# A retention and ELU kernel: a gate before the first weight load, PSUM tiles of the turn split by copying engine, and a redrawn order around the value scaling

## The chip, the cores and the metric

The kernel runs on one core of a Trainium2 chip. The metric is the device time of one execution in microseconds (us). TensorE (PE in the profile) multiplies matrices, VectorE (DVE), ScalarE (ACT) and GpSimd (POOL) do elementwise work, and SyncE (SP) issues DMAs. DMAs are issued from SyncE, GpSimd and, for some outputs, ScalarE; they share the core's 16 DMA engines. Those that convert float32 to bfloat16 on the way are issued from GpSimd. PE writes its results to PSUM, from which VectorE and ScalarE read.

## The reference

Retention over 8 batches of 8 heads, 576 positions and a head size of 64, followed by a two-layer network with an ELU between the layers, on 4608 tokens of 512 features (hidden size 2048):

```python
scores = scale * np.matmul(q, k.transpose(0, 1, 3, 2))
gamma = 1.0 - 2.0 ** (-5.0 - np.arange(H, dtype=np.float32))
rel = pos[:, None] - pos[None, :]
Dmat = np.where(rel >= 0, gamma[:, None, None] ** rel[None, :, :], 0.0)
attn = np.matmul(scores * Dmat[None], v)               # B, H, S, D
x = attn.transpose(0, 2, 1, 3).reshape(B * S, H * D)
h = x @ w_in
g = np.where(h > 0.0, h, np.exp(np.minimum(h, 0.0)) - 1.0)
out = g @ w_out
```

## The kernel before, in words

The 4608 tokens are 36 units of 128. The decay factors into a part for the keys, which is multiplied into the values (`gk`, `gkp`), and a part for the queries, which is multiplied into the attention output (`gx`); within a unit a 0/1 mask is applied to the scores, and across units a running state of 64 by 64 per head is carried. The attention output `xt` is already turned, so that it feeds the first layer as it is. Units form groups of at most four. `f1(g, n)` is a tile of the first layer for group g: matmuls with `w_in_sb` into a PSUM bank `ph` (L544), then on ScalarE `e = exp(ph)` (L549), on GpSimd `m = e - 1` (L551) and on VectorE `g = min(max(ph, 0), m)` (L524). The second layer multiplies `g` by `w_out_sb` (L569, L600), copies, and stores. A bank of `ph` is free again once its `g` is made.

The order of instructions on every engine is the order in which the program writes them. Each engine works through its own queue strictly in that order, so an instruction that waits holds up what stands behind it on its engine; the tile layer puts the waits in. VectorE's `g` is written three tiles after its matmuls (`finish(3)` in `tick`), so that its place among VectorE's other work follows from the order of the `f1` calls.

The change concerns the first four units. They are handled as two pairs: pair 0 is units 0 and 1, pair 1 is units 2 and 3, each with 256 positions of the first sequence in all 8 heads. What happens to a pair s:

- its keys and queries are loaded. For pair 0 in float32 on SyncE, two halves of four heads each (`rawk`, `rawq`, L130), and cast to bfloat16 by VectorE (first half) and ScalarE (second half), L625 to L630. For pair 1 directly as bfloat16 on GpSimd (`pair_qk`, L119);
- its values are loaded in float32 (`pair_v`, L124): on SyncE for pair 0, on GpSimd for pair 1, each in two halves;
- `pair_scale` (L358, GpSimd) multiplies the values by the keys' decay, two instructions;
- `pair_turn_in(s, c)` (L375) turns the keys (c = 1) or queries (c = 0) on PE in two parts a = 0, 1 of eight transposes each, and `pair_turn_out` (L383, L385) copies a part to SBUF, with `V` (VectorE) or `A` (ScalarE). Before the change all four parts of a pair stand in one PSUM tile `tr`, and the tile layer orders the engines that touch it;
- `pair_scores(s, a)` (L397) multiplies queries by keys into `psc`, and VectorE masks the result (L403) to `ppt`; a = 0 uses the PSUM tag "o", a = 1 the tag "sc";
- `pair_states` (L415) and `pair_state_out` (L444, L440 on ScalarE) make the states, `pair_intra` (L468) and `pair_inter` (L457) the outputs, and `pair_x` (L479, VectorE) the x of the pair, on which group s of the first layer starts.

Between them PE runs dummy matmuls (`dummy`, L218) on a tile of zeros. The weights are loaded on GpSimd: `load_w_in(n)` (L105) brings a quarter of w_in, enough for four 128-wide hidden tiles, in two DMAs; `load_w_out` (L108) half of w_out in one. `f1(0, 0)` and `f1(0, 1)` use quarter 0, `f1(0, 2)` and `f1(0, 3)` quarter 1, `f1(0, 4)` and `f1(0, 5)` quarter 2; quarter 3 and w_out are used after the first eight tiles of groups 0 and 1. There are three `ph` banks; a tile that names `m` uses the bank "pm" in place of one.

The PSUM pools: "ph" of three banks, "pm" of one, "sc" and "o" of two banks each, all handed out in turn, with a wait until the last reader of the previous user is done.

Of the kernel before, what the change touches and what calls it, by code (L numbers as in the profile page):

```python
# [9 lines left out]
FP32 = mybir.dt.float32  # L10
BF16 = mybir.dt.bfloat16
# [6 lines left out]
def kernel(  # L18
# [9 lines left out]
    nc = tc.nc  # L28
    PSUM = bass.MemoryType.PSUM

    B, H, S, D = q.shape
    DM, DF = moe_w_in.shape
    P = 128
    HP = H // 2
# [24 lines left out]
    const = ctx.enter_context(tc.tile_pool(name="const", bufs=1))  # L59
# [10 lines left out]
    ps_h = ctx.enter_context(tc.tile_pool(name="ps_h", bufs=3, space=PSUM))  # L70
    ps_m = ctx.enter_context(tc.tile_pool(name="ps_m", bufs=1, space=PSUM))
    ps_s = ctx.enter_context(tc.tile_pool(name="ps_s", bufs=1, space=PSUM))
    ps_o = ctx.enter_context(tc.tile_pool(name="ps_o", bufs=1, space=PSUM))
# [28 lines left out]
    def load_w_in(n):  # L102
        s = slice(n * 512, (n + 1) * 512)
        for b in range(2):
            nc.gpsimd.dma_start(w_in_sb[b * 64 : b * 64 + 64, :, s], w_in_v[b, :, :, s])  # L105

    def load_w_out(f0, f1):
        nc.gpsimd.dma_start(w_out_sb[:, f0:f1], w_out_v[:, f0:f1])  # L108
# [3 lines left out]
    def pair_runs(x, s, h0, h1):  # L112
        return x[0, h0:h1, 2 * P * s : 2 * P * (s + 1), :].rearrange("h (p e) d -> p h (e d)", e=2)

    pq, pk_, pv, pvn, pT, ppt, pst = {}, {}, {}, {}, {}, {}, {}

    def pair_qk(s, x, kept):
        kept[s] = qkpool.tile([P, H, 2 * D], BF16, name="pqk", tag="qkn")
        nc.gpsimd.dma_start(kept[s], pair_runs(x, s, 0, H))  # L119

    def pair_v(s, queue):
        pv[s] = [raw.tile([P, HP, 2 * D], FP32, name="pv", tag="rv") for b in range(2)]
        for b in range(2):
            queue.dma_start(pv[s][b], pair_runs(v, s, b * HP, (b + 1) * HP))  # L124


    rawk, rawq = ([opool.tile([P, HP, 2 * D], FP32, name="rqk", tag="ot") for b in range(2)] for c in range(2))
# [15 lines left out]
    for h in range(H):  # L143
        b, j = divmod(h, KJ)
# [25 lines left out]
    for c in range(2):  # L170
        nc.gpsimd.iota(
            pk_i[c * 64 : (c + 1) * 64, R + 4 : R + 6], pattern=[[1, 2]], base=-MID, channel_multiplier=2
        )
    load_w_in(0)
    pair_qk(1, q, pq)
    pair_qk(1, k, pk_)
    pair_v(1, nc.gpsimd)

    pk = const.tile([P, R + 6], FP32, name="pk")
    nc.vector.tensor_copy(pk, pk_i)  # L180
    ident = const.tile([P, P], BF16, name="ident")
# [30 lines left out]
    def dummy(n, bank=None):  # L212

        if n:
            pool, tag = bank or (ps_m, "pm")
            dum = pool.tile([P, 512], FP32, name="dum", tag=tag)
        for _ in range(n):
            nc.tensor.matmul(dum, warm[:, :P], warm, start=True, stop=True)  # L218
# [136 lines left out]
    def pair_scale(s):  # L355
        pvn[s] = [nat.tile([P, HP, 2, D], BF16, name="pvn", tag="vn") for b in range(2)]
        for b in range(2):
            nc.gpsimd.tensor_tensor(  # L358
                pvn[s][b], pv[s][b].rearrange("p h (e d) -> p h e d", e=2),
                gkp[:, s, b * HP : (b + 1) * HP].unsqueeze(3).to_broadcast([P, HP, 2, D]), ALU.mult,  # L360
            )

    def pair_turn_in(s, c):


        if (s, "tr") not in pT:
            pT[s, "tr"] = ps_s.tile([P, 2, 2, 2, 2, P], BF16, name="tr", tag="sc")
            pT[s] = [tpool.tile([P, 2, 2, 2 * P], BF16, name="pT", tag="qkT") for a in range(2)]
        n = (pq, pk_)[c][s]
        for a in range(2):  # L370
            part = pT[s, "tr"][:, a, c] if s == 0 else pT[s, "tr"][:, c, a]
            for j in range(2):
                for e in range(2):
                    for b in range(2):
                        nc.tensor.transpose(  # L375
                            part[b * D : (b + 1) * D, j, e], n[:, b * HP + 2 * a + j, e * D : (e + 1) * D], ident
                        )

    def pair_turn_out(s, c, a, copy):

        part = pT[s, "tr"][:, a, c] if s == 0 else pT[s, "tr"][:, c, a]
        if c:
            copy(pT[s][a][:, 1], part.rearrange("p j e t -> p j (e t)"))  # L383
        else:
            copy(pT[s][a][:, 0].rearrange("p j (t e) -> p j e t", e=2), part)  # L385

    def pair_scores(s, a):

        pool, tag = ((ps_o, "o"), (ps_s, "sc"))[a]
        sc = pool.tile([P, 2, 2, 2, P], FP32, name="psc", tag=tag)  # L390
        t = pT[s][a]
        for j in range(2):
            for e in range(2):
                for c in range(2):
                    for b in range(2):
                        r = slice(b * D, (b + 1) * D)
                        nc.tensor.matmul(  # L397
                            sc[c * 64 : (c + 1) * 64, b, j, e],
                            t[r, 1, j, e * P + c * 64 : e * P + (c + 1) * 64], t[r, 0, j, c * P : (c + 1) * P],
                            start=(j == 0 and e == 0), stop=(j == 1 and e == 1), skip_group_check=True,  # L400
                        )
        pt = ppool.tile([P, 2, 2, 2, P], BF16, name="ppt", tag="pt")
        nc.vector.tensor_tensor(  # L403
            pt.rearrange("p b j e t -> p (b j) e t"), sc.rearrange("p b j e t -> p (b j) e t"),
            maskp.unsqueeze(1).to_broadcast([P, 4, 2, P]), ALU.mult,
        )
        ppt[s, a] = pt

    def pair_state(out, s, rows, layout, first):

        for j in range(HP):
            for e in range(2):
                for b in range(2):
                    h = 4 * b + j if layout == "b" else 2 * j + b
                    nc.tensor.matmul(  # L415
                        out[b * D : (b + 1) * D, j], pk_[s][rows, h, e * D : (e + 1) * D],
                        pvn[s][h // HP][rows, h % HP, e],
                        start=(first and j == 0 and e == 0), stop=(j == HP - 1 and e == 1), skip_group_check=True,
                    )

    def pair_states(s):

        unit = slice(0, 64)
        if s == 0:
            pst[1] = ps_h.tile([P, HP, D], FP32, name="pst", tag="ph")
            both = ps_m.tile([P, 2, HP, D], FP32, name="pst2", tag="pm")
            pst[2], pst[4] = both[:, 0], both[:, 1]
            pst[3] = pst[2]
            pair_state(pst[1], 0, unit, "b", True)
            pair_state(pst[2], 0, slice(0, P), "b", True)  # L430
            pair_state(pst[4], 0, slice(0, P), "", False)
        else:
            pair_state(pst[3], 1, unit, "b", False)
            pair_state(pst[4], 1, slice(0, P), "", False)

    def pair_state_out(u):

        if u == 4:
            sbs[u] = ppool.tile([P, HP, D], BF16, name="sb", tag="sb")
            nc.scalar.copy(sbs[u], pst[u])  # L440
            return
        for b in range(2):
            r = slice(b * D, (b + 1) * D)
            nc.scalar.copy(sbd[u - 1][r, :, r], pst[u][r])  # L444

    def pair_outputs(s):
        if s == 0:
            for u in range(2):
                os_[u] = ps_h.tile([P, HP, P], FP32, name="po", tag="ph")
        else:  # L450
            o = ps_o.tile([P, 2, HP, P], FP32, name="po", tag="o")
            os_[2], os_[3] = o[:, 0], o[:, 1]
# [22 lines left out]
    def pair_x(s):  # L475
        xts[s] = xpool.tile([P, KJ, 512], BF16, name="xt", tag="xt")
        for c in range(2):
            s0 = (2 * s + c) * P
            nc.vector.tensor_tensor(  # L479
                xts[s][:, :, c * P : (c + 1) * P], os_[2 * s + c], gx[:, :, s0 : s0 + P], ALU.mult  # L480
            )
# [135 lines left out]
    h, m = (ps_h, "ph"), (ps_m, "pm")  # L617
# [5 lines left out]
    spare = (ps_o, "o")  # L623
# [11 lines left out]
    pair_turn_out(0, 0, 0, V)  # L635
    pair_turn_out(0, 0, 1, A)
    pair_scale(0)
    for n in range(1, 4):
        load_w_in(n)
    pair_scale(1)  # L640
    dummy(3, spare)
    pair_scores(0, 0)
    pair_scores(0, 1)
    make_gx(2, 3)
# [13 lines left out]
    def f1(g, n, bank=None):  # L658
        k = 512 // (P * len(GROUPS[g]))
        ffn1(g, k * n, bank, (g, n) == (0, 0))  # L660
# [4 lines left out]
    for c, copy in ((1, V), (0, A)):  # L665
        for a in range(2):
            pair_turn_out(1, c, a, copy)
    f1(0, 1)
    load_w_out(0, 8)
    load_w_out(8, 16)  # L670
    pair_scores(1, 0)
    pair_states(1)
    pair_state_out(3)
    pair_scores(1, 1)
    f1(0, 2)
    pair_outputs(1)
    pair_intra(1, 0)
    pair_inter(2)
# [1 line left out]
    pair_inter(3)  # L680
    pair_x(1)
    pair_state_out(4)
    f1(0, 3)
    f1(0, 4, m)
    f1(0, 5)
    make_mask()
# [51 lines left out]
    for g in range(3, NG + 1):  # L738
# [6 lines left out]
        a, b = 0, 1 if g == 4 else 0  # L745
# [80 lines left out]
```

## Time and profile before

| what | value |
|---|---|
| median of 4 runs | 317.09 us |
| lowest and highest run | 316.65 and 318.78 us |
| the profiled execution: time and span | 316.79 us and 315.0 us |
| PE, PE weight loads | 304.2 us (97%), 167.8 us (53%) |
| VectorE, ScalarE, GpSimd | 179.8 (57%), 126.2 (40%), 198.5 us (63%) |
| DMA moved | 41.12 MB, mean 131 GB/s |
| gaps of PE over 0.6 us after its first instruction | 2.71 us ahead of 10.12, 0.69 ahead of 22.82, 1.23 ahead of 76.37 |

The span is from the first to the last instruction; the time of a run has what lies around it too. Lines such as L375 are lines of the kernel before; in the changed kernel they stand a few lines lower. In the timeline and in the chain of waits the first number is the start in us, the second the duration; in brackets stands how long the engine was idle ahead of the instruction and what ended that. In the windows each row is a stretch of time with each engine's busy time and number of instructions, then the granted PE clock as a share of full speed, the DMA share and GB/s.

### The profile page before, as it was taken

How to read it: one execution, taken by the hardware profiler on the slowest of the kernel's cores; microseconds unless marked ns; L12 is line 12 of the kernel's file. 1: busy time of each engine (PE TensorE's matmuls, PEld its weight loads, DVE VectorE, ACT ScalarE, POOL GpSimd, SP SyncE). 2: the span in 40 equal slices, each digit the busy share in tenths (PEclk: the TensorE clock that was granted, in tenths of full speed). 3: DMA queues.
4: the chain of work that ended last, by engine and by line, in shares of the span. 5: the costliest groups of instructions: out<-in, count | busy, mean ns of one | idle time of the engine just before them, and what ended most of it. 6: DMA issues, size and time to landing. Idle time of an engine off the chain costs nothing.

```text
span 315.0 us, 7512 instructions
## 1 busy us (share of the span) xinstructions
PE 304.2 (97%) x3006; PEld 167.8 (53%) x3006; DVE 179.8 (57%) x303; ACT 126.2 (40%) x229; POOL 198.5 (63%) x287
## 2 busy tenths in 40 slices
PE   7799999998999999999999999999999999999995
PEld 2377745876766555555444444444444444444444
DVE  5339625686766777577666555565556555434300
ACT  4445602442443444344434433444344433444411
POOL 8276887697977878877777666776664433333300
PEclk9599999999999999999999999999999999999999
DMA  7999999999999999999999999999996200000111
GB/s 160 218 168 164 200 127 186 191 137 184 213 154 172 153 165 154 160 126 159 143 144 133 144 134 135 133 135 134 115 154 85 67 35 35 35 33 33 69 67 68
DMA packets 145827, 41.12 MB, mean 131 GB/s; under 512 B 133632, under 2 KB 141184, under 8 KB 145792
## 3 DMA queue, kind: packets, MB, share of 16 engines
q0 software_dynamic: 73184, 13.64, 53.8%
q1 hardware_dynamic: 71168, 24.72, 42.2%
q10 hardware_dynamic: 1440, 2.29, 2.3%
q8 instruction: 23, 0.38, 0.5%
q14 instruction: 12, 0.10, 0.1%
HBM read 36.70 MB, written 9.44 MB: 146 GB/s over the span
## 4 chain that ended last, share of the span: by engine, by line
PE 87%; DMA 4%; DVE 4%; ACT 1%; POOL 1%; issue 1%; SPq 0%; ACTq 0%; POOLq 0%; DVEq 0%
PE ph L544 35%; PE pm L569 33%; PE pm L600 4%; PE o L349 3%; PE sc L261 3%; DMA rqk<-in_q_dram 2%; DMA qkT<-qkn 2%; PE dum L218 1%; POOL m L551 1%; DVE g L524 1%; PE o L300 1%; PE o L316 1%; PE pmh L585 1%; DVE pt L278 1%; PE tr L375 1%
## 5 line engine op out<-in xcount | busy, mean ns | idle before, releaser
L551 POOL TENSOR_SCALAR m<-e 128x512 bf16<-128x512 f32 (+1 forms) x152 | 90.3, 596 | 89.9 <-ACT e L549 81.5
L544 PE MATMUL ph<-xt,w_in_sb 128*128 128x512 bf16 (+3 forms) x840 | 145.8, 312 | 0.8 <-DVE rv L82 0.4
L549 ACT ACTIVATE e<-ph 128x512 f32<-128x512 f32 (+1 forms) x152 | 87.3, 575 | 142.0 <-PE ph L544 134.3
L524 DVE SCALAR_TENSOR_TENSOR g<-ph,m 128x512 bf16<-128x512 f32 (+1 forms) x152 | 99.5, 659 | 60.9 <-POOL m L551 60.8
L569 PE MATMUL pm<-w_out_sb,g 128*128 128x512 bf16 x496 | 125.6, 379 | 0.2 <-ACT ot L576 0.2
L544 PEld LDWEIGHTS <-w_in_sb 128*128 128x128 bf16 x840 | 74.3, 98 | 52.3 <-issue 1.7
L569 PEld LDWEIGHTS <-g 128*128 128x128 bf16 x496 | 48.0, 98 | 53.1 <-issue 0.4
L491 DVE TENSOR_TENSOR xt<-o,gx 128x512 bf16<-128x512 f32 x32 | 22.1, 690 | 35.9 <-PE o L316 30.6
L278 DVE TENSOR_TENSOR pt<-sc,mask 128x1024 bf16<-128x1024 f32 x32 | 38.9, 1214 | 3.1 <-PE sc L261 3.1
L226 POOL TENSOR_TENSOR vn<-rv,gk 128x512 bf16<-128x512 f32 x32 | 33.3, 1041 | 3.0 <-PE ph L544 1.9
L93 POOL DMA_DIRECT2D qkn<-in_q_dram x36 | 32.1, 893 | 0.7 <-DVE pt L278 0.4
L93 POOL DMA_DIRECT2D qkn<-in_k_dram x36 | 30.7, 853 | 0.0
L576 ACT COPY ot<-pm 128x512 f32<-128x512 f32 x31 | 18.1, 585 | 14.1 <-PE pm L569 14.1
L261 PEld LDWEIGHTS <-qkT 64*64 64x64 bf16 x512 | 8.0, 106 | 13.1 <-issue 10.5
L261 PE MATMUL sc<-qkT 64*64 64x128 bf16 (+1 forms) x512 | 13.2, 211 | 1.4 <-DMA qkT<-qkn 1.2
L600 PE MATMUL pm<-w_out_sb,g 128*128 128x512 bf16 x64 | 14.5, 379 | 0.0
L349 PE MATMUL o<-pt,vn 128*64 128x128 bf16 x256 | 13.2, 225 | 0.0
L218 PE MATMUL dum<-warm 128*128 128x512 bf16 x26 | 10.5, 556 | 1.2 <-DVE warm L136 1.2
L300 PE MATMUL o<-qkT,sb 64*64 64x128 bf16 (+1 forms) x232 | 10.2, 215 | 0.4 <-DVE rv L82 0.4
L600 PEld LDWEIGHTS <-g 128*128 128x128 bf16 x64 | 6.1, 98 | 6.8 <-issue 0.2
L349 PEld LDWEIGHTS <-vn 128*64 128x64 bf16 x256 | 8.1, 109 | 2.7
L316 PE MATMUL o<-vn,qkn 128*64 128x64 bf16 (+1 forms) x224 | 8.2, 196 | 0.0
(76 smaller groups left out, 113.9 us busy)
## 6 DMA issues: line engine op xcount, KB each, us to landing
rv<-in_v_dram SPq DMA_DIRECT2D x28, 256.0 KB, 5.0
out_dram<-ot SPq DMA_DIRECT2D x27, 256.0 KB, 2.4
qkn<-in_q_dram POOLq DMA_DIRECT2D x28, 128.0 KB, 5.3
qkn<-in_k_dram POOLq DMA_DIRECT2D x28, 128.0 KB, 5.2
w_in_sb<-in_moe_w_in_dram POOLq DMA_DIRECT2D x8, 256.0 KB, 7.3
w_out_sb<-in_moe_w_out_dram POOLq DMA_DIRECT2D x2, 1024.0 KB, 12.2
out_dram<-ot ACTq DMA_DIRECT2D x8, 256.0 KB, 4.9
rv<-in_v_dram SPq DMA_DIRECT2D x8, 128.0 KB, 4.1
```

Of the source, the lines that this page charges most:

```text
L93: nc.gpsimd.dma_start(kns[u][p0 : p0 + n, c], (q, k)[c][b, :, s0 : s0 + n, :].rearrange("h p d -> p h d"))
L226: nc.gpsimd.tensor_tensor(vns[u], raws[u], gk[:, u % R].unsqueeze(2).to_broadcast([P, H, D]), ALU.mult)
L261: nc.tensor.matmul(sc[j * 64 : (j + 1) * 64, i, hp, c], t[r, 1, hp, j * 64 : (j + 1) * 64], t[r, 0, hp, c], start=(hp == 0), stop=(hp == H ...
L278: nc.vector.tensor_tensor(pts[u][:, s].rearrange("p i h t -> p (i h) t"), scs[u][:, s].rearrange("p i h t -> p (i h) t"), m.unsqueeze(1).t ...
L349: nc.tensor.matmul(o[b * D : (b + 1) * D, i, a * P : (a + 1) * P], vns[u][:, h], pts[u][:, i, 2 * b + a], start=(u % R == 0 and a == 0), s ...
L491: nc.vector.tensor_tensor(xts[g][:, :, i * P : (i + 1) * P].rearrange("p (a i) t -> p a i t", a=2), outputs(os_[u]), gx[:, :, s0 : s0 + P] ...
L524: nc.vector.scalar_tensor_tensor(gt_, ph, 0.0, m, ALU.max, ALU.min)
L544: nc.tensor.matmul(ph[:, i * n + c : i * n + c + step], w_in_sb[:, j, f : f + P], xts[g][:, j, c : c + step], start=(j == 0), stop=(j == K ...
L549: nc.scalar.activation(e[:, w], ph[:, w], AF.Exp)
L551: nc.gpsimd.tensor_scalar(m[:, w], e[:, w], -1.0, 1.0, ALU.add, ALU.mult)
L569: nc.tensor.matmul(pm, gts[g, ft][:, it * P : (it + 1) * P], w_out_sb[:, ft], start=(ft == 0), stop=(ft == NFT - 1))
L600: nc.tensor.matmul(acc[u], gts[g, ft][:, it * P : (it + 1) * P], w_out_sb[:, ft], start=(ft == 0), stop=(ft == NFT - 1))
```

## The change

- A one-element copy on GpSimd, `gate`, reads the second half of pair 0's keys, ahead of the first `load_w_in`. GpSimd's following instructions stand behind it.
- `pair_v(1)` on GpSimd moves from behind the `pair_qk` loads to behind `pair_scale(0)`.
- Of the three `load_w_in` behind it, quarters 1 and 2 stay ahead of `pair_scale(1)`; quarter 3 moves ahead of `f1(0, 1)`. The halves of w_out move from behind `f1(0, 1)` to behind `f1(0, 2)` and behind `f1(0, 3)`.
- The turned parts of a pair no longer share one PSUM tile. Pair 0: the two parts of the keys are tiles of "ph", those of the queries are tiles of "sc" (copied by VectorE) and "o" (copied by ScalarE). Pair 1: the keys stand in "sc" (both copied by VectorE), the queries in "o" (both copied by ScalarE).
- `dummy(3, spare)` ahead of the first scores moves to the bank "pm".
- For pair 1 the second scores follow the first directly, ahead of the states; `f1(0, 2)` moves from behind them to behind `pair_x(1)`. With that the first `g` on VectorE stands behind `pair_x(1)`, not ahead of it.

```diff
@@
+    gate = const.tile([1, 1], FP32, name="gate")
+    nc.gpsimd.tensor_copy(gate, rawk[1][0:1, 0, 0:1])
     load_w_in(0)
     pair_qk(1, q, pq)
     pair_qk(1, k, pk_)
-    pair_v(1, nc.gpsimd)
@@ def pair_turn_in(s, c):
         if (s, "tr") not in pT:
-            pT[s, "tr"] = ps_s.tile([P, 2, 2, 2, 2, P], BF16, name="tr", tag="sc")
+            pT[s, "tr"] = {}
             pT[s] = [tpool.tile([P, 2, 2, 2 * P], BF16, name="pT", tag="qkT") for a in range(2)]
         n = (pq, pk_)[c][s]
+        sc, o, h = (ps_s, "sc"), (ps_o, "o"), (ps_h, "ph")
         for a in range(2):
-            part = pT[s, "tr"][:, a, c] if s == 0 else pT[s, "tr"][:, c, a]
+            pool, tag = (h if c else (sc, o)[a]) if s == 0 else (sc if c else o)
+            if s == 0 or a == 0:
+                part = pool.tile([P, 2, 2, 2, P], BF16, name="tr", tag=tag)
+            pT[s, "tr"][c, a] = part[:, a if s else 0]
...
 def pair_turn_out(s, c, a, copy):
-        part = pT[s, "tr"][:, a, c] if s == 0 else pT[s, "tr"][:, c, a]
+        part = pT[s, "tr"][c, a]
@@
     pair_scale(0)
-    for n in range(1, 4):
-        load_w_in(n)
+    pair_v(1, nc.gpsimd)
+    load_w_in(1)
+    load_w_in(2)
     pair_scale(1)
-    dummy(3, spare)
+    dummy(3, m)
     pair_scores(0, 0)
@@
             pair_turn_out(1, c, a, copy)
+    load_w_in(3)
     f1(0, 1)
-    load_w_out(0, 8)
-    load_w_out(8, 16)
     pair_scores(1, 0)
+    pair_scores(1, 1)
     pair_states(1)
     pair_state_out(3)
-    pair_scores(1, 1)
-    f1(0, 2)
     pair_outputs(1)
     pair_intra(1, 0)
     pair_inter(2)
@@
     pair_x(1)
     pair_state_out(4)
+    f1(0, 2)
+    load_w_out(0, 8)
     f1(0, 3)
+    load_w_out(8, 16)
     f1(0, 4, m)
```

More of the change, by code (lines that the diff above doesn't have):

```diff
@@ L375, in pair_turn_in @@
                         nc.tensor.transpose(
-                            part[b * D : (b + 1) * D, j, e], n[:, b * HP + 2 * a + j, e * D : (e + 1) * D], ident
+                            pT[s, "tr"][c, a][b * D : (b + 1) * D, j, e],
+                            n[:, b * HP + 2 * a + j, e * D : (e + 1) * D], ident,
                         )
     def pair_turn_out(s, c, a, copy):
-        part = pT[s, "tr"][:, a, c] if s == 0 else pT[s, "tr"][:, c, a]
+        part = pT[s, "tr"][c, a]
         if c:
```

## The prediction

> All times are microseconds from the start of the profiled span of the kernel before. "Front" is everything up to the turn of the second pair (the first 32 transposes of L375 that start at 20.07), "back" is from there to the fourth tile of the first layer, f1(0,3).
>
> **What bounds the kernel now.** I read the page's slices first: TensorE is at 97%, nearly full from the fourth slice to the last, so a change can pay only where TensorE has gaps or runs slowly, and the slices put both into the first 30 us. Then the chain of waits, in order of time:
>
> ```profile
> 2.33 6.62 DMA rqk<-in_q_dram
> ...
> 8.97 0.62 ACT pqk L630
> 9.59 0.49 ACT pT L383
> ...
> 10.12 1.07 PE tr L375 x16
> ...
> 12.64 1.07 PE psc L397 x28
> 13.71 1.82 PE dum L218 x4
> 15.53 0.73 PE po L468 x14
> ```
>
> The start hangs on the second half of the first pair's q, which is 6.62 us under way. The dummies before 15.53 hide another wait, shown by the timeline of GpSimd: the second value tile is only scaled at 14.57, after its DMA.
>
> ```profile
> 14.57 1.04 POOL L358 TENSOR_TENSOR pvn<-pv,gk 128x512 bf16<-128x512 f32 x1 [0.60 <-DMA pv<-in_v_dram]
> ```
>
> Next the view of DMA issues, one issue at a time (last column: issue to landing), and the windows of 1 us (last columns: granted clock, DMA share, GB/s):
>
> ```profile
> rqk<-in_k_dram SPq DMA_DIRECT2D x1, 256.0 KB, 2.9
> rqk<-in_q_dram SPq DMA_DIRECT2D x1, 256.0 KB, 6.6
> pv<-in_v_dram SPq DMA_DIRECT2D x1, 256.0 KB, 11.1
> pqk<-in_k_dram POOLq DMA_DIRECT2D x1, 256.0 KB, 11.8
> ```
>
> ```profile
> 3.00:4.00 1.00, 1.00 (x4) 0.34 (x3) 0.74 (x4) 0.84 (x2) 0.99 (x3) 1.00 1.08 313
> 4.00:5.00 1.00, 1.00 (x3) 0.30 (x2) 0.92 (x3) 0.49 (x1) 1.00 (x2) 1.00 0.94 266
> 6.00:7.00 1.00, 1.00 (x19) 0.59 (x18) 0.20 (x2) 0.00 (x0) 1.00 (x2) 1.00 0.79 126
> 10.00:11.00 1.00, 0.88 (x16) 0.82 (x15) 0.00 (x0) 0.07 (x1) 0.00 (x0) 0.50 1.24 212
> ```
>
> SyncE's queue alone moves some 276 GB/s (249, 313 and 266 from 2 to 5). From about 5.4 on, 2.9 after GpSimd issues the first w_in part at 2.50, the total falls to 113 to 141, and the second q half and the values (landed 8.95, 12.8, 14.55) crawl. The clock is half from about 9.4 to 16.2, after TensorE's gap of 2.71 us ahead of 10.12.
>
> **The gate, and pair_v(1) moved back.** The gate waits for the second half of k, landed 4.4; with about 0.1 for a one-element copy (the memsets' 0.10 on GpSimd is the nearest row) w_in is issued from 4.6. Queued behind it on GpSimd are w_in (1.46) and the two pqk loads (0.92, 0.89): done at 7.9. First bytes: rows give 2.9 (w_in) and at least 2.3 (w_out, issued at 24.47, its rate back only after 26 to 27); I take 2.9, so 7.5. By 5.0 the windows add to 845 KB; six loads of 262 KB are 1573, so the 728 left take 2.64 at 276 GB/s: all through at 7.6, just as the rival stream starts. Landings run some 0.5 behind the bytes: q at 5.3 and 6.3, values at 7.3 and 8.2, instead of 5.7, 8.95, 12.8, 14.55. If only 2.3 hold, the last value half shares for 0.6 us and lands up to 1 later, still under GpSimd's own order.
>
> The Trainium skill, DMA: Bandwidth & Descriptors, Specifications, puts the first byte of a GpSimd DMA at about 1 us. By that the second stream would start at 5.7 and share with half of q and both value tiles; an estimate from it puts the scaled values near 13 and takes most of the gain away. The 2.9 of this trace decides.
>
> **TensorE from there, duration by duration.** Twelve dummies, the k transposes and two dummies end at 7.41, as now. The second q half is cast by 7.0 (0.62), so the q transposes run at 7.4 to 8.0 (0.56 at full clock, as the k ones). VectorE and ScalarE copy (0.73 each) together to 8.75, since each has its own tile. Scores 8.8 to 9.6; VectorE masks (1.22 each) to 10.5 and 11.7. GpSimd scales (1.04 twice) from 7.9 to 10.0. So the products of L468 start at 10.5, limited by the mask, not at 15.46. From there to f1(0,0) took 3.47, of which some 0.4 was half clock; the rest of the order is kept, so 2.9 to 3.1, f1(0,0) at 13.5 and its end with the x halves at 14.6. TensorE keeps no gap like the 2.71, so the clock holds.
>
> The second pair's k is needed at 14.6. The GpSimd stream must move 1049 KB (w_in part, two pqk) from 7.5. At 177 GB/s, the mean of the windows 17 to 26, where it runs alone, it lands at 14.0; with pqk as slow as now (4.2 from w_in landed to k landed) at 15.2. I take 14.7. Bounds: 200 GB/s (windows 21 to 24) gives 13.3, hidden; the whole present interval of 14.2 from issue gives 18.85. Front: 20.07 - 14.7 = **5.4 won** (5.5 to 1.2).
>
> **Separate turn tiles.** For the first pair they are in the sum: the serial pair of copies of 0.73 (ScalarE's began at 12.06, after VectorE's end) becomes parallel. In exchange psc(0,0) in "o" waits for ScalarE's copy as well, no later than VectorE's.
>
> The skill, PSUM — Partial Sum Buffer, Specifications (TRN2), says that ScalarE and VectorE may read PSUM in parallel if their banks differ. The two halves lay in different banks before, yet the row shows them one after the other; by the rule alone splitting wins nothing here, by the row 0.73.
>
> **Second pair redrawn (back).** Before, 20.07 to 26.55 = 6.48, f1(0,2) inside. After: turn 1.05; two ScalarE copies 1.32 with latencies, 1.45, as psc(1,0) waits for both; scores to mask 0.47; two masks 2.36; then intra and inter 0.7; f1(0,2) hides under pair_x (1.29), but f1(0,3) takes the bank of f1(0,0), and VectorE's order puts that g (0.68) behind pair_x. Sum 1.05 + 1.45 + 0.47 + 2.36 + 0.75 + 1.3 + 0.7 = 8.1: **1.6 lost**. It was f1(0,2) under the masks and g ahead of pair_x that covered this. With g earlier (not so in the order) 0.7 would come back; I keep 1.3 to 1.9.
>
> **DMA issues on GpSimd.** Before the second scaling there are six, as before (2 x 0.78 + 4 x 0.65 = 4.1 for 3.73), from 10.0 to 14.2. pv(1) lands behind pqk, 0.7 and 1.6 later as now: 16.3; scaled by 17.4, needed by the states near 18. w_in parts 1 and 2 follow at 1.2 to 1.5 a piece: 19 and 22, needed at 21 and 24. w_in part 3 (1.3 on GpSimd) delays m(0,1) to 19.5, not needed before g at 22.7. w_out issues (0.95 each) go at 23 and 25, behind m(0,2) and m(0,3), against 24.47 and 25.4; they land near 33 and 39, needed at 35 and 42. They push one m by about 0.3, against the waits of 0.23 and 0.42 that TensorE has now at 28.3 and 33.9: zero, 0.5 either way. If they landed over 2 later than that, TensorE would wait for them one for one. The three dummies moved from the "o" to the "pm" bank cost nothing: they stay in TensorE's own order, and "pm" is free until the states.
>
> **Sum.** 5.4 - 1.6 - 0.1 = 3.7. The profiled execution took 316.79, span 315.0 and 1.8 around it: 313.1. The median shown is 0.3 above it, so 317.09 - 3.7 = **313.4**.
>
> **The rivals.** *A: the gain is eaten by the transfers behind it.* The w_out loads move forward by only 0.5 to 1.5, units 4 to 7 queue behind them, and TensorE already waits 1.23 at 75.14 for a transposed tile. Against: unit 4's last key part lands at 42.7 for a turn at 47.3, unit 5's at 48.7 for 52.6, so 3.8 to 4.6 spare for a difference of 2.2 to 3.2. If it holds, about half the gain stays: 315.2.
>
> *B: slower, since the second pair's values come late.* pair_v(1) now stands behind the scaling; with the present 11.7 from issue (now 10.0 and 10.8) the second half lands at 22.5, is scaled at 23.6, states 0.82, sbd 0.74, inter 0.4, pair_x 1.29, g 0.68: f1(0,3) at 27.6 against 26.55, so 318.1. It decides from a landing of 21.4 on. For it: every m on GpSimd queues behind that wait, and q0 is busy. Against: the 11.7 were spent behind six other loads, four of which will be through.
>
> *C: the gate does not free the queue:* q still lands near 9 since something else limits it. Then 0.5 to 0.9 from the parallel copies, less 1.6: 317.9. Against: the first three halves came 0.8 to 1.3 apart.
>
> **How the numbers follow.** A measurement of this kernel tells about 0.5% (1.6 us) from no change. Forecast 0.75, with its own range 312.0 to 315.0; A 0.13, B 0.07, C 0.05. To leave two in ten out at most and take in the unknowns (front down to 3, the wait at 75 gone or doubled), 311.6 to 316.0. Faster needs under 315.5: the forecast and half of A, 0.82; same 0.12 (rest of A, most of B and C); slower 0.06.
>
> **What would show it.** Second q half landing near 6.3, last value half near 8; half clock absent after 6; L468 starting near 10.5; turn of the second pair near 14.7; f1(0,3) near 22.8 with a wait for VectorE's g of about 1 us before it; a steady lead of about 3.7 from 30 to 300. Wrong it is if the q half lands after 8, if pqk lands after 17, or if a lead at 30 is gone at 80.

## The result, and the profile after

| | before | changed |
|---|---|---|
| median | 317.7 us (64 runs) | 315.39 us (43 runs) |
| ratio, with its 95% interval | | 0.9925, 0.991 to 0.994 |
| profiled execution: time, span | 316.79, 315.0 us | 315.08, 313.3 us |
| turn of the second pair starts | 20.07 | 16.07 |
| f1(0,3) starts | 26.38 | 24.16 |
| the first-layer tile that waits 0.42 for VectorE's `rv` (L82) starts | 34.34 | 32.71 |

The change gains some 2.4 us (0.75%), 1.7 in the two profiled executions. The last three rows are places that every kernel below passes, so the gain can be followed: 4.0 us at the turn, 2.2 at f1(0,3), 1.6 at the `rv` tile, 1.7 at the end. Two of the profiles below are of slower executions, that of *best_full* at a granted clock of 0.56 throughout and that of *mask_early* at 319.41 us where the median is 315.07, and no time of theirs is compared with others.

The three places in TensorE's timeline before (start, duration; the second line begins with f1(0,3)):

```profile
20.07 1.08 PE L375 MATMUL tr<-ident,pqk 128*64 128x128 bf16 x32
26.38 1.91 PE L544 MATMUL ph<-xt,w_in_sb 128*128 128x256 bf16 x16
34.34 4.53 PE L544 MATMUL ph<-xt,w_in_sb 128*128 128x256 bf16 x40 [0.42 <-DVE rv L82]
```

The chain of waits of the changed kernel in order of time (start, duration, what):

```profile
1.25 4.08 DMA rqk<-in_k_dram
5.38 0.18 POOL gate L175
5.56 0.78 POOL w_in_sb L105
6.97 0.90 POOL pqk L119
7.87 8.15 DMA pqk<-in_k_dram
16.07 1.10 PE tr L379 x32
...
27.26 1.48 DVE mask L210 x2
28.87 2.38 DVE g L529 x4
32.71 4.53 PE ph L549 x40
```

The first pair's q is gone from the chain. In its place stand k's landing, the gate, GpSimd's issues, and the transfer of the second pair's keys, 8.15 under way. Later two masks and four `g` of VectorE are on it; the chain of before had two `g` there and no mask.

The DMA issues of the changed kernel, single ones (last column: issue to landing):

```profile
rqk<-in_q_dram SPq DMA_DIRECT2D x1, 256.0 KB, 4.8
pv<-in_v_dram SPq DMA_DIRECT2D x1, 256.0 KB, 6.3
pqk<-in_k_dram POOLq DMA_DIRECT2D x1, 256.0 KB, 8.2
```

The second q half takes 4.8 instead of 6.6, the second value half 6.3 instead of 11.1, the second pair's keys 8.2 instead of 11.8. The windows of 1 us show why (last three columns: granted clock, DMA share, GB/s):

```profile
6.00:7.00 1.00, 0.98 (x17) 0.59 (x17) 0.76 (x2) 0.00 (x0) 0.99 (x3) 1.00 1.17 317
8.00:9.00 1.00, 1.00 (x18) 0.47 (x12) 0.74 (x1) 0.76 (x2) 1.00 (x2) 1.00 0.99 140
12.00:13.00 1.00, 1.00 (x36) 0.53 (x30) 0.07 (x1) 0.95 (x4) 1.00 (x3) 1.00 1.71 165
```

SyncE's queue keeps its rate until 7 (317 GB/s, before 126 in this window), and has 0.11 MB left when the first bytes of GpSimd's stream come, at 7.05. The granted clock is full in all three, as it is in every window of this profile.

TensorE's timeline in the changed kernel (start, duration; in brackets the idle time ahead):

```profile
10.99 0.42 PE L473 MATMUL po<-ppt,pvn 64*64 64x128 bf16 x16
16.07 1.08 PE L379 MATMUL tr<-ident,pqk 128*64 128x128 bf16 x32 [0.85 <-DMA pqk<-in_k_dram]
24.16 4.53 PE L549 MATMUL ph<-xt,w_in_sb 128*128 128x256 bf16 x40 [1.10 <-DVE g L529]
29.51 2.78 PE L549 MATMUL ph<-xt,w_in_sb 128*128 128x256 bf16 x24 [0.82 <-DVE g L529]
```

The first products start at 10.99 (before 15.46). Three waits of over 0.6 are new: 0.85 for the keys, 1.10 and 0.82 for VectorE's `g`.

### The profile page after: what moved, and what is told of

The parts are those of the page before. It is cut to its first block, busy times and chain, and to the rows that moved or that the text cites. A ratio compares the mean times of both kernels' runs of the same rounds, so it can differ in the third digit from the quotient of the medians.

```text
span 313.3 us, 7511 instructions
## 1 busy us (share of the span) xinstructions
PE 301.3 (96%) x3006; PEld 166.8 (53%) x3006; DVE 180.1 (57%) x303; ACT 126.3 (40%) x229; POOL 198.5 (63%) x288
## 4 chain that ended last, share of the span: by engine, by line
PE 84%; DMA 6%; DVE 4%; POOL 2%; issue 1%; ACT 1%; SPq 0%; POOLq 0%; DVEq 0%; ACTq 0%
PE ph L549 35%; PE pm L574 33%; PE pm L605 4%; PE o L350 3%; PE sc L262 3%; DMA pqk<-in_k_dram 3%; DMA qkT<-qkn 2%; DVE g L529 2%; DMA rqk<-in_k_dram 1%; PE o L301 1%; PE o L317 1%; PE pmh L590 1%; POOL m L556 1%; DVE pt L279 1%; DVE mask L210 0%
## 5 line engine op out<-in xcount | busy, mean ns | idle before, releaser
L262 PEld LDWEIGHTS <-qkT 64*64 64x64 bf16 x512 | 8.0, 106 | 13.1 <-issue 10.5
L262 PE MATMUL sc<-qkT 64*64 64x128 bf16 (+1 forms) x512 | 13.2, 211 | 1.5 <-DMA qkT<-qkn 1.3
L350 PE MATMUL o<-pt,vn 128*64 128x128 bf16 x256 | 13.2, 225 | 0.0
L219 PE MATMUL dum<-warm 128*128 128x512 bf16 x26 | 8.1, 448 | 1.2 <-DVE warm L136 1.2
```

The costliest lines, as they stand in the source:

```text
L262: nc.tensor.matmul(sc[j * 64 : (j + 1) * 64, i, hp, c], t[r, 1, hp, j * 64 : (j + 1) * 64], t[r, 0, hp, c], start=(hp == 0), stop=(hp == H ...
L350: nc.tensor.matmul(o[b * D : (b + 1) * D, i, a * P : (a + 1) * P], vns[u][:, h], pts[u][:, i, 2 * b + a], start=(u % R == 0 and a == 0), s ...
```

## The experiments

Each edit is made on the changed kernel, unless it says otherwise, and each ratio is to the kernel before, timed in five rounds on the same chip. The changed kernel was profiled and timed a second time beside the second set.

| run | turn | `rv` tile | span | ratio, interval |
|---|---|---|---|---|
| before | 20.07 | 34.34 | 315.0 | |
| changed | 16.07 | 32.71 | 313.3 | 0.9925, 0.991 to 0.994 |
| after_again | 15.19 | 32.34 | 312.7 | 0.9902, 0.9866 to 0.9938 |
| no_gate | 19.10 | 35.76 | 316.6 | 1.0079, 1.0043 to 1.0115 |
| gate_only | 16.20 | 30.68 | 311.8 | 0.9915, 0.9886 to 0.9944 |
| one_tr | 16.36 | 33.28 | 313.5 | 0.9962, 0.9938 to 0.9986 |
| cover | 14.82 | 30.90 | 311.6 | 0.9898, 0.9863 to 0.9934 |
| mask_early | | | | 0.9910, 0.9870 to 0.9951 |
| half_w | 15.16 | 33.51 | 314.0 | 0.9909, 0.9870 to 0.9948 |
| cover_pv_mask | 15.84 | 31.26 | 314.4 | 0.9876, 0.9819 to 0.9932 |
| gate_first | 15.52 | 32.93 | 313.4 | 0.9952, 0.9917 to 0.9987 |
| best_half | 15.39 | 30.32 | 313.2 | 0.9896, 0.9854 to 0.9938 |
| best_full | | | | 0.9940, 0.9913 to 0.9968 |
| best_qk9 | 15.67 | 30.69 | 310.1 | 0.9816, 0.9778 to 0.9854 |

**after_again: the changed kernel itself.** 

> The changed kernel as it is, on the same chip as the next three, as their anchor: about 2.4 us below before; the turn of the second pair between 15.5 and 16.2, when its keys land.

Keys land at 15.0 rather than 16.05, so over a microsecond of the front differs between two executions of one kernel. What it wins there goes to a wait of 1.06 of the states for `pvn`, the scaled values, and a half clock from 20.3 to 23.7 behind it.

**no_gate and gate_only: which part does it.** The first takes these two lines out of the changed kernel, the second adds them to the kernel before:

```diff
+    gate = const.tile([1, 1], FP32, name="gate")
+    nc.gpsimd.tensor_copy(gate, rawk[1][0:1, 0, 0:1])
     load_w_in(0)
```

> The changed kernel without the gate: w_in is issued near 2.5 again, all else as changed. Theory 1 (the gate wins the front, because without it GpSimd's loads share the DMA engines with the first pair's q and values): the second q half lands near 9 and not near 7, the last value half near 14, the clock is half for some 7 us, the second pair's turn starts near 19.5, and with the 1.6 us that the new order costs behind it the time is about 1 us above the kernel before. Rival (the split turn tiles or the new order brought the gain): the time stays about 2 us below before.

> The kernel before with the gate alone: pair_v(1) and the w_in parts stay where they were, the turn shares one PSUM tile, the order of the second pair is the old one. Theory 1: the front is won as in the changed kernel (turn of the second pair near 16, since its keys land then), and the old order behind it loses nothing, so about 3.5 us below before, more than the whole change. Rival (the gate needs the moved pair_v or the split tiles, without which values or turned parts come late): 1 us below before or less.

The DMA issues of no_gate (second q half, second value half):

```profile
rqk<-in_q_dram SPq DMA_DIRECT2D x1, 256.0 KB, 6.6
pv<-in_v_dram SPq DMA_DIRECT2D x1, 256.0 KB, 10.3
```

One window of no_gate:

```profile
6.00:7.00 1.00, 1.00 (x14) 0.57 (x14) 0.00 (x0) 0.00 (x0) 0.00 (x0) 1.00 0.92 126
```

The same two DMA issues in gate_only:

```profile
rqk<-in_q_dram SPq DMA_DIRECT2D x1, 256.0 KB, 4.9
pv<-in_v_dram SPq DMA_DIRECT2D x1, 256.0 KB, 6.1
```

And the same window in gate_only:

```profile
6.00:7.00 1.00, 0.78 (x12) 0.29 (x7) 0.83 (x2) 0.00 (x0) 1.00 (x2) 1.00 1.10 323
```

The gate alone decides the rate of SyncE's queue: 126 GB/s without it and 323 with it in the same window. Without it the change is slower than before by 0.8% (2.5 us); with it alone the old order is faster by 0.85%. In the profile of no_gate the wait for q is 1.50 where it was 2.71, and no half clock follows, though one was expected; but the second value half, landed at 13.7, brings 1.38 before the products. That profile has the highest mean clock of its seven executions, 1.0; the others have 0.984 to 0.995.

The traces also price the redrawn order. From the turn to the `rv` tile before takes 14.27 and gate_only 14.48; the changed kernel takes 16.64 and no_gate 16.66. So the order, with the moved loads and split tiles that came with it, costs 2.2 to 2.4 at that place, with the gate or without it. The times of gate_only and the changed kernel cannot be told apart all the same. Part of the early lead is lost between: gate_only waits 1.77 for a transposed tile at 73.28, the changed kernel 1.27 at 74.79. In gate_only's span, 1.5 shorter than the changed kernel's, 1.5 of the 2.0 led at the `rv` tile is left.

**one_tr: the split of the turned tiles undone.** The part that picks the tile goes back:

```diff
-            pT[s, "tr"] = {}
+            pT[s, "tr"] = ps_s.tile([P, 2, 2, 2, 2, P], BF16, name="tr", tag="sc")
...
-            part = pool.tile([P, 2, 2, 2, P], BF16, name="tr", tag=tag)
+            part = pT[s, "tr"][:, a, c] if s == 0 else pT[s, "tr"][:, c, a]
```

> The changed kernel with one PSUM tile for all turned parts of a pair, as before: theory: the split is hidden behind the wait for the second pair's keys (0.85 us of idle TensorE in the changed kernel), so the first pair loses 0.7 us that nobody waits for and the second pair 0.2; the time is within 0.3 us of the changed kernel, about 2.2 below before. Rival (the split is worth its 0.73 on the path): 1.7 below before or less, and TensorE's first L473 and the turn of the second pair both 0.7 later.

From TensorE's waits (waiting line, for what: us in total, times, longest) of one_tr:

```profile
PE tr L376 <- ACT pT L384: 1.8, 1, 1.8
```

The q transposes wait until the last copy of the keys has left the shared tile, and the first products start at 12.21 instead of 10.99. In the span only 0.2 of it is left, since in the changed kernel the keys hold up the turn until 16.07, and one_tr comes to it at 16.36 without a wait; by the ratios the split is worth 1.2 us (0.9962 less 0.9925), with intervals that touch and from different sets. The expectation of no more than 0.3 holds for the profiled execution but not for the times.

**cover: f1(0,2) back under the masks.**

```diff
     pair_state_out(3)
+    f1(0, 2)
     pair_outputs(1)
...
     pair_state_out(4)
-    f1(0, 2)
     load_w_out(0, 8)
```

> The changed kernel with f1(0,2) put back under the masks, ahead of the second pair's outputs, so that its g is also ahead of pair_x on VectorE. Theory: the stretch from the second pair's turn to f1(0,3) falls from 8.1 to about 6.3 us, the waits of 0.40, 0.38 and 1.10 us in it shrink or go, and the time is some 1.5 us below the changed kernel, 3.9 below before. Rival (VectorE's g and masks or w_in's landing limit the stretch anyway): less than 0.5 us below the changed kernel.

TensorE's waits between 8 and 28 in cover:

```profile
PE ph L549 <- issue: 1.2, 1, 1.2
PE pst L420 <- POOL pvn L359: 1.0, 1, 1.0
```

From the turn to the `rv` tile it takes 16.08 instead of 16.64, though two waits are in it that the first profile of the changed kernel did not have, 2.3 together. Less these it would be 13.8, no longer than before's 14.27. By this subtraction, an estimate, one moved call is most of what the redrawn order costs there. The values become the next limit when the keys come early. The times do not show the 1.5 us that were expected: 0.9898 is not told apart from the changed kernel's 0.9925 and 0.9902.

**mask_early: VectorE's masks at a quiet time.** `make_mask()` moves from behind `f1(0, 5)` to behind `make_maskp()`:

```diff
     make_maskp()
+    make_mask()
...
     f1(0, 5)
-    make_mask()
```

> The changed kernel with make_mask() moved to directly behind make_maskp(), when VectorE waits for the first pair's q. Theory: in the changed kernel the two mask instructions took 1.55 us between three m of GpSimd, where before they took 0.47, and TensorE waited 0.82 us for the g behind them; moved, that wait goes and the time is 0.8 us below the changed kernel (0.5 to 1.0). Rival (the wait at that place comes from GpSimd's m, delayed by the w_out issues between them): the wait stays 0.5 or more and the time is within 0.3 us.

The masks in VectorE's timeline, before and in the changed kernel:

```profile
29.57 0.47 DVE L209 TENSOR_SCALAR mask<-px,pk 128x128 bf16<-128x128 f32 x2
27.17 1.55 DVE L210 TENSOR_SCALAR mask<-px,pk 128x128 bf16<-128x128 f32 x2
```

TensorE's waits from 24 to 36 in the changed kernel:

```profile
PE ph L549 <- DVE g L529: 1.9, 2, 1.1
PE ph L549 <- DVE rv L82: 0.4, 1, 0.4
```

The masks in VectorE's timeline of mask_early:

```profile
4.48 0.48 DVE L210 TENSOR_SCALAR mask<-px,pk 128x128 bf16<-128x128 f32 x2
```

TensorE's waits from 24 to 36 in mask_early:

```profile
PE ph L549 <- DVE rv L82: 0.4, 1, 0.4
PE ph L549 <- DVE g L529: 0.3, 1, 0.3
```

The two masks take 0.48 where no `m` of GpSimd runs beside them, 0.47 in the kernel before, where one `m` runs beside their first 0.1, and 1.55 in the changed kernel, where three `m` run from 27.43 to 29.21. With them away, the wait of 0.82 is gone. That execution has other waits: states wait 1.28 and 0.88 for `pvn`, and the clock is half from 23.5 to 26.9 and, behind a wait of 2.54 for a transposed tile, from 78.1 to 81.5. The 0.8 us that were expected do not appear: 0.9910 is not told apart from the 0.9902 of the changed kernel in the same set.

**half_w: half the weights ahead of the keys.** Only the columns that f1(0,0) uses stay ahead of `pqk`; those of f1(0,1) come later:

```diff
-    load_w_in(0)
+    load_w_cols(0, 256)
     pair_qk(1, q, pq)
...
     pair_scale(0)
+    load_w_cols(256, 512)
```

> The changed kernel with only half of the first w_in part (256 of its 512 columns, all that f1(0,0) uses) ahead of the second pair's q and k; the other half follows behind the first value scaling. Theory (the front is now bound by the landing of the second pair's keys, in the order of GpSimd's own stream): they land some 1.3 us earlier, near 14.7, TensorE's 0.85 us of waiting for them goes, and the time falls by 0.6 to 0.9 us against the changed kernel, unless f1(0,1) now waits for its half. Rival (the keys' landing is set by the total traffic, not by their place in the stream, since transfers of one queue progress together): they land within 0.5 us of the changed kernel and so does the time.

The DMA issue of the second pair's keys in half_w:

```profile
pqk<-in_k_dram POOLq DMA_DIRECT2D x1, 256.0 KB, 6.0
```

The longest of TensorE's waits from 10 to 28 in half_w:

```profile
PE pst L424 <- POOL pvn L363: 1.8, 1, 1.8
```

The keys land at 13.2, and the turn at 15.16 no longer waits for them. The values, behind one more load, make the states wait 1.80, and the clock is half from 22.06 to 25.48. A second landing has taken the place of the first, and the time, 0.9909, is not told apart from the changed kernel's either.

**cover_pv_mask: cover, early masks, and pair_v(1) back behind the pqk loads.**

```diff
     pair_qk(1, k, pk_)
+    pair_v(1, nc.gpsimd)
...
-    pair_v(1, nc.gpsimd)
     load_w_in(1)
```

> The version with f1(0,2) under the masks, with two more edits: pair_v(1) back directly behind the second pair's q and k, and make_mask() behind make_maskp(). Theory: TensorE's wait of 1.04 us for the second pair's scaled values goes, since they land by about 16.5; the time is 0.7 to 1.2 us below the cover version, some 4.8 below before. Rival (the values' early place delays the first pair's scaling by 1.5 us, and that is on the path): no better than the cover version.

The stretch from turn to `rv` tile is 15.42; the states still wait 0.85 for the values. The wait for a transposed tile has grown to 2.19, with half clock from 75.3 to 78.7 behind it. The times show no gain over cover (0.9876 and 0.9898), where 0.7 to 1.2 us were expected.

**gate_first: the gate on the first half of k.**

```diff
-    nc.gpsimd.tensor_copy(gate, rawk[1][0:1, 0, 0:1])
+    nc.gpsimd.tensor_copy(gate, rawk[0][0:1, 0, 0:1])
```

> The changed kernel with the gate on the first half of k (landed 3.6) in place of the second (4.6 to 5.4). Theory: w_in is issued near 3.8, its stream starts near 6.7, when SyncE's queue still holds about a fifth of its bytes, so the last value half lands up to 1.5 later, which nobody waits for, and the second pair's keys about 1 earlier: within 0.5 us of the changed kernel, rather below. Rival (every us of sharing costs the first pair as much as it did without the gate): the last value half lands past 11 and the time is 1 us or more above the changed kernel.

The first w_in part is issued at 4.15 instead of 5.51, yet the keys land at 15.5, between the changed kernel's 15.0 and 16.05. In the trace the stream does not start earlier. Its first bytes come at 7.29, and at 7.05 in the changed kernel; until then only SyncE's queue moves bytes, and the last value half lands at 9.2, no later than the changed kernel's 9.7. Nothing is won by it.

**best_full, best_half, best_qk9: what is left.** All have cover and mask_early, and `pair_v(1)` on SyncE behind `pair_v(0)`; `load_w_in(2)` stands behind `pair_scale(1)`. best_half adds half_w. best_qk9 adds to best_half that the queries and keys of unit 9 are loaded earlier on GpSimd:

```diff
     load_v(8, nc.vector)
+    load_qk(9)
...
     state_out(5)
-    load_qk(9)
     load_v(9, nc.vector)
```

> The changed kernel with f1(0,2) under the masks, make_mask() behind make_maskp(), and the second pair's values on SyncE's queue behind the first pair's (pair_v(1, nc.sync) at the start), so that GpSimd's stream holds only w_in and the second pair's q and k; pair_scale(1) goes ahead of w_in part 2. Theory (what bound the second pair behind its keys was its values, 17 to 19 us in GpSimd's stream): they land near 11, TensorE's waits of about 1 us at L420 go; the second pair's keys land within 1 us of before this edit; f1(0,3) starts near 22 and the time is about 5 us below before. Rival (SyncE's longer stream holds up GpSimd's): the second pair's keys land 1.5 us or more later, and the gain over the cover version (3.2 below before) is nil.

> The same with half of the first w_in part behind the first value scaling. Theory: the keys land some 2 us earlier than in the version with all of it ahead, near 14, and TensorE comes to the second pair's turn without a wait; a further 0.5 to 1 us below, some 5.5 to 6 below before. Rival: f1(0,1) then waits for its half of the weights, or for its instructions, and nothing is left of it.

> The version with half of w_in first, the second pair's values on SyncE, f1(0,2) under the masks and make_mask() early, with unit 9's q and k loads issued directly behind unit 8's, where GpSimd is idle for some 4 us, in place of some 9 us later. Theory: TensorE's wait near 72 for unit 9's turned tile (1.23 us in the kernel before, 1.0 to 2.6 in the others, longer the further the start had been brought forward) goes or falls under 0.5, with it the half clock of 3.4 us that followed it in the profile of the version without this edit; the lead at 30 (4.0 us there) is kept to the end: 4 to 5 us below before. Rival (the transposes are held up by the traffic as a whole, or the next unit's takes the wait over): 1 us or more of waiting for a turned tile stays between 65 and 85, and the time is as without this edit, some 3.3 us below before.

In best_half the values land at 10.3 and 12.7, and no wait for `pvn` is left. The longest of TensorE's waits from 28 to 95 in best_half:

```profile
PE sc L267 <- DMA qkT<-qkn: 1.9, 1, 1.9
```

Two windows of best_half (granted clock third from the end):

```profile
70.00:74.00 4.00, 2.06 (x51) 1.49 (x48) 1.31 (x2) 0.68 (x2) 2.23 (x4) 1.00 1.98 163
74.00:78.00 4.00, 4.00 (x22) 2.35 (x19) 3.37 (x5) 0.60 (x1) 2.65 (x4) 0.57 1.67 195
```

It leads the changed kernel by 2.4 at the `rv` tile (30.32 against 32.71) and by 0.1 at the end. The wait at 71 to 73 and the slow clock behind it, 74.30 to 77.72, take the lead. The transposition waited for is issued on SyncE at 65.78, after 6.0 of waiting for loaded keys. All of TensorE's waits from 28 to 95 in best_qk9:

```profile
PE ph L554 <- DVE rv L82: 0.4, 1, 0.4
PE o L306 <- DVE rv L82: 0.4, 1, 0.4
PE sc L267 <- DVE sc L276: 0.2, 1, 0.2
```

The same transposition is issued at 60.84; no wait for it is left, and the clock stays full. This kernel is faster than the kernel before (311.82 against 317.56 in the same set, 5.8 us by the ratio) and than the changed kernel; its interval just touches that of best_half, which was timed in another set. best_full and best_half fell short of what was expected, with 1.9 and 3.3 us by the ratios. best_full, without half_w, is less good than best_half in the medians, with intervals that overlap; why is not settled.

## Why the prediction was right, and where it was not

- **The gate and its mechanism: right.** SyncE's queue keeps its rate, 317 GB/s from 6 to 7, and the loads behind it follow; no_gate and gate_only show that nothing else does it. The second q half landed at 7.1 for 6.3, the last value half at 9.7 for 8.2, the products began at 10.99 for 10.5 and f1(0,0) at 14.01 for 13.5. The second half of k, and with it the gate, came at 5.35 in that execution, not 4.4, but that is not the reason: in after_again and half_w the gate ran at 4.7, and q, the products and f1(0,0) came at 7.1 to 7.2, 11.0 and 14.0 to 14.1 all the same. The term that was mis-sized is the landing behind the bytes, put at 0.5. By the windows' sums (an estimate) the bytes of the second q half had passed at 5.7, and SyncE's last bytes passed at 8.3; both landings came 1.4 later. No half clock after 6: right in this profile, not in after_again.
- **The front, 5.4 won: mis-sized, 4.0 measured.** This is the step of the sum that failed. The keys were put at 14.7; they landed at 16.05, at 15.0 in after_again and at 15.5 to 15.7 in gate_first, one_tr and gate_only. Of the 1.4 that are missing, 0.85 is the wait for them, and the rest is f1(0,0), 0.5 late. The issue of w_in at 5.51 instead of 4.6 is not the cause, since the first bytes came at 7.05, earlier than the 7.5 put. Nor is it the rate: from 7.05 to 16.05 the queue moved 1.51 MB, which is 168 GB/s, where 177 had been used. The amount was too small: the prediction had the keys land with the 1049 KB of w_in, q and k, but these had passed only together with over 0.4 MB of the second pair's values, which stood behind the keys on the queue and moved from 13.5 on, while the keys' last bytes passed at 15.7. In after_again it was 1.5 MB as well. How much earlier the keys would land without them was not tried by itself; best_half has the values on SyncE, but its first bytes come later, at 7.93. half_w confirms that what stands ahead of the keys in GpSimd's stream set the turn: with 0.13 MB less for each of two loads they came at 13.2. The 16.05 lies within the bounds given, 13.3 to 18.85.
- **The first bytes of GpSimd's stream.** Working with 2.9, read from windows of 1 us, was right in direction; what was measured after the issue of w_in is 1.54 in the changed kernel, 2.48 in the kernel before, and 2.1 to 3.1 in the others. No fixed time after the issue fits: in the nine profiles with the gate and the values of pair 0 alone on SyncE, w_in was issued between 4.15 and 5.51, and the first bytes came between 6.9 and 7.3, when SyncE's queue had 0.11 to 0.19 MB left. What sets that was not tried. The Trainium skill, DMA: Bandwidth & Descriptors, Specifications, states about 1 us; every run here lies above it.
- **The back, 1.6 lost: right, 1.8 measured.** Turn to f1(0,3) took 8.09 for 8.1, with a wait of 1.10 for `g` as foreseen. The old stretch was read 0.17 too long: 26.55 is the end of the piece ahead of f1(0,3) in the chain of waits, and f1(0,3) starts at 26.38, so that it took 6.31 and not 6.48. gate_only keeps the old order and takes 6.31 too. That it is f1(0,2) under the masks that is lost is argued from cover, less its two new waits; it is not shown by itself.
- **The waits after that, zero with 0.5 either way: wrong.** 0.6 more was lost (2.2 led at f1(0,3), 1.6 at the `rv` tile) in the wait of 0.82 for a `g` that stands behind `make_mask`. The masks moved under GpSimd's `m`, and take 1.55 instead of 0.47. mask_early, with the masks elsewhere, has no such wait, though its times show no gain. VectorE's other work at that place was not in the working at all.
- **Split tiles: right in kind.** Parallel copies were put at 0.73; one_tr shows 1.2 at the first products, and between 0.2 (span) and 1.2 (times) at the end.
- **Rival A, eaten by later transfers: not here, but near.** The lead of 1.6 at 33 is 1.7 at the end, and the wait at 75 is 1.27 for 1.23. Where the lead at 30 is larger, in best_half, this rival is what happens, and best_qk9, without that wait, keeps it.
- **Rival B, the values late: not decisive, yet real.** The last value half landed near 17.7 in the changed kernel, far from 21.4, and the changed kernel has no wait for it when the keys land at 16.05. When they land earlier (after_again, cover, half_w) the states wait 1.0 to 1.8 for the scaled values.
- **Rival C falls:** q and the values came as the gate let them.

By the ledger of the two profiles: 4.0 - 1.8 - 0.6 = 1.6, and 1.7 at the end, against 5.4 - 1.6 - 0.1 = 3.7. By the ratio 2.4 were gained. Counted from the 317.09 that the prediction started from, that is 314.7, inside the forecast's own 312.0 to 315.0; the median of 315.39 is inside the outer range alone, beside the 315.2 of rival A, whose mechanism did not happen. So the mechanism was right and the size was not: a third of the gain is missing, in the front and in a wait that the sum did not have.

## What to carry to other kernels

When two DMA queues share the engines, a one-element copy that holds back the later-needed stream can be worth more than a redrawn order: here it was the whole gain. Price a landing by all that its queue will have moved by then, what is queued behind it included, and then ask which transfer is due next, because a lead of 1 to 3 us was eaten twice, by the values at 20 and by a transposed tile at 73. When an instruction list is redrawn, look also at small work of the other engines that falls into a new place.

## What the runs showed of the hardware

- **Half clock after short gaps.** Stretches of half clock of about 3.4 us followed gaps of TensorE of 1.06 (after_again), 1.80 (half_w), 1.95 (best_half), 2.19 (cover_pv_mask) and 2.54 (mask_early), and began 0.7 to 1.8 after the gap's end; in the kernel before the clock fell at 9.4, when TensorE had stood still for 2.0 of its 2.71. None followed gaps of 1.27 (changed kernel), 1.50 (no_gate), 1.65 and 1.77 (gate_only). The length of a gap alone doesn't decide; what does was not tried. The mean clock of single executions adds to what the gate is worth: it is 0.982 to 0.995 in all 82 of the kernel before that were run beside the experiments, and 0.998 or more in 30 of 43 of the changed kernel, in 7 of 11 of gate_only and in 1 of 7 of no_gate. The median of the 30 is 315.1 us; that of the changed kernel's nine at 0.993 to 0.995 is 316.7. One stretch of 3.4 at half clock takes 1.7 of 315 us off, or 0.005 of the clock (an estimate), so these nine have about one each. The Trainium skill, TensorE: Matmul & The Clock Gate, What's actually happening, gives an idle window of about 3.4 us for going slow and as much busy time for coming back; the stretches have that length, but no gap here was that long.
- **VectorE beside GpSimd.** Two mask instructions took 0.48 without an `m` of GpSimd beside them (mask_early) and 1.55 with three (changed kernel). The Trainium skill, SBUF — State Buffer, SBUF: two separate sides, says that the two engines lock a shared pair of ports for whole instructions, and the other one waits; of VectorE's instructions it says so for those in a two-port mode or with two SBUF inputs. The numbers agree with such a wait; whether the mask is an instruction of that kind, no run here shows.
- **Stalls without a releaser.** In eight of the profiles TensorE stood still ahead of a first-layer tile with nothing that the trace names, from 0.38 (gate_only) and 0.48 (one_tr) to 1.10 (gate_first) and 1.24 (cover). Each ended 2.4 to 2.9 after the start of a 16 KB instruction transfer (14.60 to 17.37 in cover). In the changed kernel such a transfer starts at 14.04, and no such stall follows. That they belong together was not tested.
